# A one-core adaLN block: doubled weights loaded in 21 pieces, wider accumulations, and a new step table

## The chip, the core and the metric

The kernel runs on one core of a Trainium2 chip. The core has a matrix engine (PE, with its weight loads shown apart as PEld), a vector engine (DVE), a scalar engine (ACT), a general engine (POOL) and a sync engine (SP) that here only issues transfers; sixteen DMA engines move the data. SBUF and PSUM have 128 partitions. The metric is the device time of one execution, in microseconds; a kernel's time is the median of its runs. A profile is one execution of its own with the profiler on. Its span runs from the first to the last instruction, and the execution's own time is a little longer.

## The reference

Sequence length S = 2048, width D = 448, 16 heads of 28, F/2 = 896, everything in bf16. Two mixers follow each other, each on a modulated layer norm, each added to x through a gate:

```python
sa, ca, ga, sb, cb, gb = split(silu(c) @ w_mod, 6)
h = layernorm(x) * (1 + ca) + sa
q, k, v = heads(h @ wqkv)
phi_q = concat(softmax(q @ w_phi), softmax(-(q @ w_phi)))    # phi_k alike
kv = einsum('bhsf,bhsd->bhfd', phi_k, v);  z = einsum('bhsf->bhf', phi_k)
o = (phi_q @ kv) / (phi_q @ z + 1e-06)
x = x + ga * (o @ wo)
h = layernorm(x) * (1 + cb) + sb
y = gelu(h @ w_in);  z1, z2 = y[:, :896], layernorm(y[:, 896:])
x = x + gb * ((z1 * (w_sp @ z2 + b_sp)) @ w_out)
```

w_sp is 2048 x 2048, w_in 448 x 1792, w_out 896 x 448.

## The kernel before

The 2048 rows are 16 tiles of 128, mostly handled as 8 pairs. D = 448 is 7 blocks of 64. A transposed pair (hT) holds, for each block, the first tile's 64 features in partitions 0 to 63 and the second tile's in 64 to 127. A matmul of a pair is therefore two matmuls of 64 rows, one in each half of PE's rows (HALF[0], HALF[1]), and the weights against which hT runs (k, q, v weights, wo, w_in) must lie in SBUF twice, once in each half of the partitions. For wv, wo and the two halves of w_in (y and z) `load_half` fetches the whole matrix into 64 partitions, and is called twice for each, so there are eight such transfers: wv0, wv1, wo0, wo1, wy0, wy1, wz0, wz1.

Nothing schedules the kernel but a table, the string ORDER: some 860 words, each a step with its arguments, engine (/Y is SP, /S ACT, /V DVE, /G POOL) and PSUM slot (@). `fast_path` runs through it and issues the steps' instructions. Each engine runs its instructions in that order, and where one waits, everything behind it on that engine waits too. Loads are words as well (ld:x1/Y). SP issues almost all transfers, so its share of ORDER is the order of the loads, of the DMA transposes (T1 for the first norm's output, T2 for the attention's output, T3 for the second norm's, W for w_sp) and of the output.

The stages that matter here, in their order:

- cf computes modulation columns with matmuls of one column (L776), ec copies them from PSUM; FT, ET, PF, EP fold w_phi into the q and k weights.
- l1s to l1a norm x; X and XE (first two pairs) or T1 and md transpose and modulate it into hT.
- The k loop, for pairs 0 to 7: kM multiplies by the k weights, kE takes both exponentials (ACT, L878), kS sums them (DVE), kR takes reciprocals, kP scales (DVE or POOL, L895), vM multiplies by wv, vC copies the result, kA adds phi_k^T v into one PSUM accumulator over all pairs (L905). kA runs the two 64-row halves as separate matmuls into two banks; kb (ACT, L910) copies the second bank to SBUF and kc (DVE, L913) adds the first, adds the small constant, and km writes the block-diagonal KVbd. qM and qE do the queries, in between.
- gr and ge make the gates ga and gb as rows; wos and wts multiply wo and w_out by them (`gate`, L947), some blocks at a time, on DVE or POOL.
- For each tile nM (PE, L960), nX, nC, nS, nV, nT (DVE, L980, into f_t, which has two buffers) divide by the normalizer; nA (POOL or DVE, L986) adds the two parts into f_oo; T2 transposes it; wX and wM (PE, L997, L1005) multiply by wo and add x; wR, wQ, lA, lD, l2r, l2a norm again; T3 transposes.
- zM (L1056) and yM (L1073) multiply by w_in, pM and its helpers do the spatial product with w_sp, oM and oE the output.
- du, dh and dk are matmuls of zeros that keep PE busy while it has nothing to do.

```python
    def load_half(eng, dst, src, h):
        eng.dma_start(out=dst[HALF[h]], in_=src.rearrange("(k p) n -> p k n", p=HB))
```

Of the kernel before, what the change touches and what calls it, by code (L numbers as in the profile page):

```python
# [9 lines left out]
ALU = mybir.AluOpType  # L10
# [5 lines left out]
P = 128  # L16
# [467 lines left out]
ld:wq/Y ld:c/S du:6@1 ld:phi/Y ld:wk/S ld:x1/Y tbl ld:x2/Y du:6@1 ld:wsa/Y ld:x0/Y ld:x3/Y du:2@1 ld:wca/Y FTq:0@0 bd:0/V ld:x4/Y m5 ct@1 bd:1/V FTq:1@2  # L484
ce:1 ETq:0/S ETq:1/V FTk:1@3 FTk:0@4 ce:2 l1s:1 ETk:1/S PFq:4@C ce:3 l1s:2 ETk:0/S l1e:1,2/G PFq:6@A1 du:2@0 l1r:1,2 ce:4 EPq:5/S l1s:3 PFk:0@A2 EPq:6/S m4
PFk:4@A0 l1s:0 l1a:1/G EPq:4/S cf:0@2 EPk:4/S l1e:2,4/V l1e:0,1/V PFq:2@C ld:wsb/Y EPk:0/S l1r:0,1 l1s:4 PFk:6@A0 du:2@3 ld:x5/Y l1a:0/G EPk:6/S l1s:5
PFk:2@A2 ld:wv1/Y EPq:3/S l1r:2,4 cf:1@3 ld:wv0/Y l1s:7 EPk:2/S l1a:3/G X:0@0 ec:0 ec:1 EPq:2/S l1s:6 PFq:0@A2 l1a:2/G ld:wcb/Y XE:0,2,4/S du:1@2 XE:0,4,6/V
scb X:1@1 XE:0,6,7/S XE:0,0,2/V l1e:4,8/G XE:1,0,2/S cf:2@2 XE:1,6,7/V l1r:4,8 l1s:8 XE:1,4,6/S kM:0@C ec:2 l1s:9 EPq:0/S l1a:5/G XE:1,2,4/S l1s:13 l1a:7/G
kE:0,1 kM:1@A1 l1a:4/G l1s:10 EPq:1/S l1a:6/G T1:2,3 l1s:11 kE:0,0 qM:0@A0 m7 l1s:12 m3 kE:1,1 T1:3,4 l1e:8,12/G kS:0,0,2 kE:1,0 qM:1@A2 l1r:8,12 ld:wmgb/Y
qE:0,0 ld:wmga/Y l1a:8/G vM:0@C kS:1,0,2 qE:0,1 l1a:10/G l1a:11/G vM:1@A1 vC:0/S l1a:9/G T1:5,6 l1s:15 qE:1,1 md:0,2,4,6,7/G cf:3@0 kR:0,0,2 md:0,2,4,1,2/G  # L490
T1:4,5 md:0,2,4,4,5/V md:0,2,4,2,3/S md:0,2,4,0,1/G md:0,2,4,3,4/V gr:1@1 md:0,2,4,5,6/S kP:0,0/G l1s:14 vC:1/S ld:wout/Y gr:0@6 W:0,0 l1e:12,16/V qE:1,0
kR:1,0,2 kM:2@A1 kP:0,1/V l1r:12,16 ge:0 kP:1,1/V kP:1,0/V md:0,4,6,6,7/G qM:2@A2 kE:2,0 l1a:15/V m6 kE:2,1 ec:3 md:0,4,6,3,4/V l1a:13/G l1a:12/V kM:3@C
ge:1 l1a:14/G kS:2,0,2 md:0,4,6,1,2/S T1:6,7 qE:2,1 vM:2@A1 md:0,4,6,5,6/G md:0,4,6,0,1/G T1:7,8 kE:3,1 md:0,4,6,2,3/G vM:3@A0 md:0,4,6,4,5/V wts:4,6/G
kR:2,0,2 kE:3,0 ld:wo0/Y vC:2/S W:0,5 kS:3,0,2 kM:4@C qE:2,0 md:0,6,8,1,2/G ld:wz0/Y qM:4@A1 md:0,6,8,0,1/G kE:4,1 md:0,6,8,3,4/G wts:2,4/V kE:4,0 ld:wo1/Y
kA:0@A2 kR:3,0,2 md:0,6,8,5,6/S kA:1@A2 md:0,6,8,6,7/V kP:2,1/G kS:4,0,2 vC:3/S kM:5@C qE:4,0 ld:wz1/Y vM:4@A0 md:0,6,8,2,3/G qE:4,1 kP:2,0/V md:0,6,8,4,5/G
# [39 lines left out]
def fast_path(tc, A_x, A_wqkv, A_w_phi, A_wo, B_w_in, B_w_sp, B_b_sp, B_w_out, c, w_mod, out, flag):  # L535
# [119 lines left out]
    def load_half(eng, dst, src, h):  # L655
        eng.dma_start(out=dst[HALF[h]], in_=src.rearrange("(k p) n -> p k n", p=HB))
# [252 lines left out]
    def kb():  # L909
        nc.scalar.copy(out=kvb, in_=ps["kv"][:, 1, 0:464])  # L910
# [394 lines left out]
```

## Time and profile before

| | us |
|---|---|
| median of 2 runs (267.71 to 267.81) | 267.76 |
| the profiled execution | 265.91 |
| its span | 264.1 |
| PE busy in the span | 238.7 |
| DVE busy | 185.0 |
| POOL busy | 127.3 |
| ACT busy | 113.7 |
| share of the span that SP's DMA queue fills on 16 engines | 51.9% |
| first kE (ACT, L878) | 23.8 |
| kb (ACT, L910) | 66.4 |
| first nA (POOL, L986) | 73.4 |
| first wM (PE, L1005) | 78.4 |
| first zM (PE, L1056) | 99.6 |

In the lines of the profile L12 is line 12 of the kernel. A group's line names line, engine, operation, the tile written and the tiles read, the count, the busy time and the mean. A line of waits names the waiting engine and line, what released it, the total, the number of times and the longest. "issue" means that the engine waited for nothing that the profile shows. A line of windows gives the stretch, the busy time of PE, PEld, DVE, ACT and POOL with instruction counts, the granted PE clock (1 is full), the busy share of the DMA engines and the GB/s they moved.

### The profile page before, as it was taken

How to read it: one execution, taken by the hardware profiler on the slowest of the kernel's cores; microseconds unless marked ns; L12 is line 12 of the kernel's file. 1: busy time of each engine (PE TensorE's matmuls, PEld its weight loads, DVE VectorE, ACT ScalarE, POOL GpSimd, SP SyncE). 2: the span in 40 equal slices, each digit the busy share in tenths (PEclk: the TensorE clock that was granted, in tenths of full speed). 3: DMA queues.
4: the chain of work that ended last, by engine and by line, in shares of the span. 5: the costliest groups of instructions: out<-in, count | busy, mean ns of one | idle time of the engine just before them, and what ended most of it. 6: DMA issues, size and time to landing. Idle time of an engine off the chain costs nothing.

```text
span 264.1 us, 6349 instructions
## 1 busy us (share of the span) xinstructions
PE 238.7 (90%) x2631; PEld 135.5 (51%) x2640; DVE 185.0 (70%) x354; ACT 113.7 (43%) x209; POOL 127.3 (48%) x147
## 2 busy tenths in 40 slices
PE   8887999993888878999799999999999999999990
PEld 6664756573864543544356544444444444544550
DVE  1955989892799977688446997449758968156650
ACT  3945899971827656799597730000001000000000
POOL 1677696970075876538447708705305281222000
PEclk9965999997959997999999999999999999999997
DMA  7998969999014795679940100009993000100032
GB/s 203 314 240 142 224 130 159 200 193 167 2 37 72 112 155 105 108 133 179 181 90 0 35 7 0 0 1 171 171 193 63 20 17 17 55 0 2 0 116 69
DMA packets 67782, 26.97 MB, mean 102 GB/s; under 512 B 55585, under 2 KB 67618, under 8 KB 67746
## 3 DMA queue, kind: packets, MB, share of 16 engines
q1 hardware_dynamic: 66992, 25.98, 51.9%
q10 hardware_dynamic: 754, 0.52, 0.7%
q8 instruction: 22, 0.36, 0.6%
q14 instruction: 14, 0.11, 0.1%
HBM read 11.22 MB, written 1.84 MB: 49 GB/s over the span
## 4 chain that ended last, share of the span: by engine, by line
PE 63%; DVE 8%; DMA 6%; POOL 6%; issue 6%; SPq 5%; ACT 4%; DVEq 0%; ACTq 0%; POOLq 0%
PE f_psum L1153 27%; PE f_psum L1103 8%; PE f_psum L1090 5%; DMA f_hx<-f_hx 5%; PE f_psum L1073 5%; PE f_psum L1056 4%; SPq L1082 3%; PE f_psum L871 3%; PE f_psum L929 3%; POOL f_hx L794 2%; PE f_psum L1005 2%; DMA f_phi<-in_A_w_phi_dram 2%; DVE f_t L980 2%; POOL f_hx L847 1%; DVE f_ksum L888 1%
## 5 line engine op out<-in xcount | busy, mean ns | idle before, releaser
L1205 POOL TENSOR_TENSOR f_z1T<-f_win,f_z1T 128x512 bf16<-128x512 f32 x10 | 13.7, 1377 | 34.2 <-DVE f_win L1180 34.2
L1153 PEld LDWEIGHTS <-f_z2n 128*128 128x128 bf16 x192 | 18.7, 98 | 22.0
L1056 PE MATMUL f_psum<-f_win,f_hx 64*128 64x448 bf16 x224 | 24.6, 368 | 3.8 <-DVE f_hx L794 1.4
L1153 PE MATMUL f_psum<-f_wsp,f_z2n 128*128 128x512 bf16 x116 | 27.3, 379 | 0.2
L1173 ACT ACTIVATE f_Eq<-f_psum 128x512 f32<-128x512 f32 x4 | 2.4, 597 | 47.8 <-PE f_psum L1153 47.8
L986 POOL TENSOR_TENSOR f_oo<-f_t 128x448 bf16<-128x448 bf16 x12 | 12.3, 1033 | 21.1 <-DVE f_t L980 21.1
L1153 PE MATMUL f_psum<-f_hx,f_Eq 128*128 128x512 bf16 x93 | 21.7, 379 | 0.2
L1073 PE MATMUL f_psum<-f_hx,f_win 64*128 64x512 bf16 x196 | 21.8, 376 | 0.0
L1103 PE MATMUL f_psum<-f_wout,f_z1T 128*128 128x448 bf16 x105 | 21.3, 352 | 0.0
L1180 DVE SCALAR_TENSOR_TENSOR f_win<-f_psum,f_win 128x512 f32<-128x512 f32 x22 | 14.7, 685 | 9.3 <-PE f_psum L1153 9.2
L1056 PEld LDWEIGHTS <-f_hx 64*128 64x128 bf16 x224 | 11.7, 98 | 15.9 <-issue 3.0
L935 ACT ACTIVATE f_Eq<-f_psum 128x1024 bf16<-128x1024 f32 x16 | 16.1, 1034 | 7.2 <-PE f_psum L929 7.2
L888 DVE TENSOR_REDUCE f_ksum<-f_E 128x64 f32<-128x1792 bf16 x8 | 15.9, 2004 | 4.4 <-ACT f_E L878 4.4
L929 PE MATMUL f_psum<-f_hx,f_Wq 64*128 64x256 bf16 x224 | 14.3, 276 | 4.3 <-issue 4.3
L871 PEld LDWEIGHTS <-f_hx 64*128 64x128 bf16 x224 | 11.6, 99 | 12.7 <-issue 4.2
L980 DVE TENSOR_TENSOR f_t<-f_psum,f_w 128x896 bf16<-128x896 f32 x16 | 16.7, 1086 | 0.4
L1073 PEld LDWEIGHTS <-f_win 64*128 64x128 bf16 x196 | 12.0, 94 | 9.1
L794 POOL TENSOR_SCALAR f_hx<-f_hx,f_mod 128x256 bf16<-128x256 bf16 x19 | 13.1, 701 | 7.0 <-DMA f_hx<-f_hx 7.0
L871 PE MATMUL f_psum<-f_Wk,f_hx 64*128 64x448 bf16 x112 | 14.4, 398 | 1.8 <-DVE f_st L835 1.6
L1176 POOL TENSOR_TENSOR f_win<-f_Eq,f_bsp 128x512 f32<-128x512 f32 x4 | 7.0, 1759 | 18.5 <-ACT f_Eq L1173 18.5
L1061 ACT ACTIVATE f_z2n<-f_psum 128x896 bf16<-128x896 f32 x16 | 14.4, 908 | 3.2 <-PE f_psum L1056 3.2
L878 ACT ACTIVATE f_E<-f_psum 128x896 bf16<-128x896 f32 x16 | 14.0, 924 | 3.6 <-PE f_psum L871 3.5
(175 smaller groups left out, 511.0 us busy)
## 6 DMA issues: line engine op xcount, KB each, us to landing
f_win<-in_B_w_in_dram SPq DMA_DIRECT2D x4, 784.0 KB, 12.7
out_dram<-f_hx SPq DMA_DIRECT2D x15, 112.0 KB, 1.8
f_wm<-in_w_mod_dram SPq DMA_DIRECT2D x4, 392.0 KB, 6.2
f_x<-in_A_x_dram SPq DMA_DIRECT2D x3, 448.0 KB, 7.3
f_wv<-in_A_wqkv_dram SPq DMA_DIRECT2D x2, 392.0 KB, 9.1
f_ka<-in_w_mod_dram SPq DMA_DIRECT2D x2, 392.0 KB, 4.8
f_wout<-in_B_w_out_dram SPq DMA_DIRECT2D x1, 784.0 KB, 5.5
f_win<-in_A_wo_dram SPq DMA_DIRECT2D x2, 392.0 KB, 7.7
```

Source lines behind the costliest of these rows:

```text
L794: eng.tensor_scalar(out=out_, in0=in_, scalar1=sc, scalar2=sh, op0=ALU.mult, op1=ALU.add)
L871: nc.tensor.matmul(t[:, h, 0:n], lhsT=hT[HALF[h], p, j, :], rhs=w[HALF[h], j, 0:n], start=(j == 0), stop=(j == NB - 1))
L888: nc.vector.tensor_reduce(out=ksum[:, 2 * p + t0:2 * p + t1], in_=Er[:, p % NR, t0:t1].rearrange("p t a s (f h) -> p (t a s) h f", h=2), a ...
L929: nc.tensor.matmul(t[:, h, u * 256:(u + 1) * 256], lhsT=Wq[HALF[h], j, 2 * c2 + u].rearrange("p h e -> p (h e)"), rhs=hT[HALF[h], 2 * st:2 ...
L935: nc.scalar.activation(out=Eq[st // 2][:, 2 * c2:2 * c2 + 2, s, o:o + 512].rearrange("p u (h q) -> p h u q", h=2), in_=ps["q" + str(n)].re ...
L980: nc.vector.tensor_tensor(out=tr[i % 2].rearrange("p s (k h d) -> p k s h d", k=2, h=8), in0=numv(i)[:, :, :, :, 0:DH], in1=wr[i // 2 % 2] ...
L1056: nc.tensor.matmul(ps["z" + str(2 * p + h)][:, hf, 0:D], lhsT=hT[HALF[h], p, j, :], rhs=win[1][HALF[h], j, hf * D:(hf + 1) * D], start=(j ...
L1061: nc.scalar.activation(out=g, in_=ps["z" + str(i)][:, :, 0:D], func=ACT.Gelu_apprx_tanh, accum_out=zs1[:, i:i + 1])
L1073: nc.tensor.matmul(t[:, h, :], lhsT=win[0][HALF[h], j, fc * P:(fc + 1) * P], rhs=hT[HALF[h], 4 * g:4 * g + 4, j, :], start=(j == 0), stop= ...
L1103: nc.tensor.matmul(ps["o" + str(t)][:, 0, 0:D], lhsT=later["z1T"][:, fc, t * P:(t + 1) * P], rhs=wout_s[:, fc, :], start=(fc == 0), stop=( ...
L1153: nc.tensor.matmul(t[:, 0, :], lhsT=b[:, j, f * P:(f + 1) * P], rhs=a[:, j, :], start=(PSTART[k] and j == 0), stop=(j == NH - 1), skip_gro ...
L1180: nc.vector.scalar_tensor_tensor(out=out_, in0=bank_, scalar=ZR, in1=other, op0=ALU.mult, op1=ALU.add)
```

## The change

It has these parts.

- Loads. `load_half` is replaced by `load_twice`: one transfer for each 64-row block of a weight, written to all 128 partitions, its source read twice through a leading dimension of 2 with step zero. wv and wo are 7 pieces each (v0 to v6, o0 to o6, 448 columns), w_in 7 pieces over y and z at once (u0 to u6, 1,792 columns): 21 transfers for 8. f_win is laid out anew for it: wo first, then y and z side by side for each block.
- kA runs one matmul of 128 rows for two of 64, in one bank: 128 matmuls for 256. kb and kc's sum are gone; kc adds the constant in PSUM, km reads PSUM.
- cf takes windows of two blocks where it can: 32 matmuls for 56, four times; ec copies two halves, 8 operations for 4.
- The zero tile is 512 wide for 256 and du's matmuls are 512 columns wide; there are 9 for 19. dk has 99 matmuls for 183. dh's 8 are gone.
- ORDER is another table. Some steps change engines (one of kP from POOL to DVE, two zQ from DVE to ACT, two cX to POOL, and the like); loads, W transposes and slots stand elsewhere.
- Four new helpers (X2, XF, X3, XO) are defined and not used by the table.

```diff
-    def load_half(eng, dst, src, h):
-        eng.dma_start(out=dst[HALF[h]], in_=src.rearrange("(k p) n -> p k n", p=HB))
+    def load_twice(eng, dst, src, k):
+        v = src[k * HB:(k + 1) * HB]
+        eng.dma_start(out=dst[:, k, :], in_=v.unsqueeze(0).to_broadcast([2, HB, v.shape[1]]))
...
+    for k in range(NB):
+        LOADS["v%d" % k] = lambda q, k=k: load_twice(q, wv, A_wqkv[:, 2 * D:3 * D], k)
+        LOADS["o%d" % k] = lambda q, k=k: load_twice(q, wo_s, A_wo, k)
+        LOADS["u%d" % k] = lambda q, k=k: load_twice(q, wyz, B_w_in, k)
...
-            nc.tensor.matmul(wps[:, 0, 0:256], lhsT=zero[:, 0:P], rhs=zero[:, 0:256], start=True, stop=True)
+            nc.tensor.matmul(wps[:, 0, :], lhsT=zero[:, 0:P], rhs=zero[:], start=True, stop=True)
...
-        for j in range(NB):
+        for w in range(NB + 1):
+            rows = HALF[1] if w == 0 else HALF[0] if w == NB else slice(0, P)
+            a, b = max(0, w - 1), min(NB, w + 1)
             for kk in range(KC):
-                for h in range(2):
-                    nc.tensor.matmul(t[HALF[h], 0, j:j + 1], lhsT=wm1[:, kk, o + j * HB:o + (j + 1) * HB], rhs=scol[:, kk:kk + 1],
-                                     start=(kk == 0), stop=(kk == KC - 1))
+                nc.tensor.matmul(t[rows, 0, w:w + 1], lhsT=wm1[:, kk, o + a * HB:o + b * HB], rhs=scol[:, kk:kk + 1], start=(kk == 0), stop=(kk == KC - 1))
...
-                for h in range(2):
-                    nc.tensor.matmul(ps["kv"][:, h, a * 58:(a + 1) * 58], lhsT=PRT[HALF[h], p % NF, t, 2 * a:2 * a + 2, :].rearrange("p a e -> p (a e)"),
-                                     rhs=VRT[HALF[h], p % NR, t, 2 * a:2 * a + 2, :].rearrange("p h f -> p (h f)"),
-                                     start=(p == 0 and t == 0 and a == 0), stop=(p == NPR - 1 and t == 1 and a == 7), skip_group_check=True)
-
-    def kb():
-        nc.scalar.copy(out=kvb, in_=ps["kv"][:, 1, 0:464])
+                nc.tensor.matmul(ps["kv"][:, 0, a * 58:(a + 1) * 58], lhsT=PRT[:, p % NF, t, 2 * a:2 * a + 2, :].rearrange("p a e -> p (a e)"),
+                                 rhs=VRT[:, p % NR, t, 2 * a:2 * a + 2, :].rearrange("p h f -> p (h f)"),
+                                 start=(p == 0 and t == 0 and a == 0), stop=(p == NPR - 1 and t == 1 and a == 7), skip_group_check=True)
 
     def kc():
-        nc.vector.tensor_tensor(out=kvb, in0=ps["kv"][:, 0, 0:464], in1=kvb, op=ALU.add)
-        z = kvb.rearrange("p (a f) -> p a f", f=29)[:, :, 28]
+        z = ps["kv"][:, 0, 0:464].rearrange("p (a f) -> p a f", f=29)[:, :, 28]
         nc.vector.tensor_scalar(out=z, in0=z, scalar1=0.5e-6, scalar2=None, op0=ALU.add)
```

Of the table, the loads of the middle of the k loop show how it reads (a row before and one now):

```diff
-kP:3,1/V kE:5,1 kA:2@A2 kM:6@A1 kR:4,0,2 kE:5,0 kP:3,0/V kP:4,1/G vC:4/S kS:5,0,2 vM:5@C kE:6,0 ld:wy1/Y kM:7@A0 kE:6,1 kP:4,0/G kR:5,0,2 vC:5/S kS:6,0,2
+kP:3,1/G ld:u0/Y kS:5,0,2 kM:6@C qE:4,1 W:0,5 wts:6,7/G kA:2@4 kE:6,1 kR:4,0,2 kA:3@4 kP:4,1/V ld:u6/Y vC:5/S kM:7@A0 kP:4,0/V kE:6,0 kR:5,0,2 ld:o0/Y
```

What SP issues before, from w_out to the first transposes of f_oo (T2); f_wsp receives blocks of w_sp, f_hx is transposed by T1, f_win holds wo and w_in:

```order
L685 DMA f_wout<-in_B_w_out_dram 128x7x448
L1082 DMA_TRANSPOSE f_wsp_84<-in_B_w_sp_dram 128x8x128
L854 DMA_TRANSPOSE f_hx<-f_hx 128x7x128 x2
L656 DMA f_win<-in_A_wo_dram 64x7x448
L1082 DMA_TRANSPOSE f_wsp_84<-in_B_w_sp_dram 128x8x128
L656 DMA f_win<-in_B_w_in_dram 64x7x896
L656 DMA f_win<-in_A_wo_dram 64x7x448
L656 DMA f_win<-in_B_w_in_dram 64x7x896 x2
L1082 DMA_TRANSPOSE f_wsp_84<-in_B_w_sp_dram 128x8x128
L656 DMA f_win<-in_B_w_in_dram 64x7x896
L854 DMA_TRANSPOSE f_oo<-f_oo 128x7x128 x4
```

And now, from the last four T1 to the same place:

```order
L856 DMA_TRANSPOSE f_hx<-f_hx 128x7x128 x4
L687 DMA f_wout<-in_B_w_out_dram 128x7x448
L658 DMA f_win<-in_B_w_in_dram 128x1x1792 x3
L688 DMA f_bsp<-in_B_b_sp_dram 128x2048
L1096 DMA_TRANSPOSE f_wsp_84<-in_B_w_sp_dram 128x8x128
L658 DMA f_win<-in_B_w_in_dram 128x1x1792 x2
L658 DMA f_win<-in_A_wo_dram 128x1x448
L658 DMA f_win<-in_B_w_in_dram 128x1x1792
L1096 DMA_TRANSPOSE f_wsp_84<-in_B_w_sp_dram 128x8x128
L658 DMA f_win<-in_B_w_in_dram 128x1x1792
L658 DMA f_win<-in_A_wo_dram 128x1x448
L856 DMA_TRANSPOSE f_oo<-f_oo 128x7x128 x2
```

All of wv and five pieces of wo stand ahead of these rows; the last piece of wo, o0, is the last load ahead of the transposes of the attention's output, and the load of f_bsp has moved here from the second half.

What POOL does before between the k loop (f_qa is kP's output) and the sums of nA (f_oo):

```order
L895 TENSOR_TENSOR f_qa<-f_E,f_kr_121 128x16x56 x2
L947 TENSOR_TENSOR f_win<-f_win,f_g_rep 128x896
L895 TENSOR_TENSOR f_qa<-f_E,f_kr_122 128x16x56
L947 TENSOR_TENSOR f_win<-f_win,f_g_rep 128x448
L986 TENSOR_TENSOR f_oo<-f_t 128x7x64 x2
```

And now, with kP at L914, the gate at L961 and nA at L1000:

```order
L914 TENSOR_TENSOR f_qa<-f_E,f_kr_122 128x16x56
L961 TENSOR_TENSOR f_win<-f_win,f_g_rep 128x896
L914 TENSOR_TENSOR f_qa<-f_E,f_kr_121 128x16x56
L961 TENSOR_TENSOR f_win<-f_win,f_g_rep 128x896
L961 TENSOR_TENSOR f_wout<-f_wout,f_g_rep 128x896
L961 TENSOR_TENSOR f_win<-f_win,f_g_rep 128x896
L1000 TENSOR_TENSOR f_oo<-f_t 128x7x64 x5
```

The second row of f_win (wos:0,2) needs the pieces o0 and o1 of wo, and POOL reaches the first nA only behind it and two further scalings.

More of the change, by code (lines that the diff above doesn't have):

```diff
@@ L528 @@
[L528 to L531 removed]
+ld:x2/Y ld:c/S m5 m4 du:4@1 ld:phi/Y ld:wk/S ld:wq/Y tbl ld:x1/Y ld:x0/Y du:2@1 ld:x3/Y ld:wca/Y l1s:3 ct@0 du:2@2 ld:wsa/Y ce:1 l1s:2 FTk:1@1 ce:2
@@ new lines @@
+kP:0,0/V qE:2,0 T1:7,8 kP:0,1/V kM:3@A0 kP:1,1/V kE:2,0 kP:1,0/V T1:6,7 qE:2,1 kA:0@4 kS:2,0,2 cf:3@5 md:0,4,6,2,3/G md:0,4,6,0,1/S ld:wout/Y md:0,4,6,3,4/G
+kE:3,0 ld:u4/Y gr:0@6 md:0,4,6,4,5/G ld:u3/Y md:0,4,6,1,2/V kE:3,1 md:0,4,6,6,7/V cf:2@7 ld:u2/Y kR:2,0,2 md:0,6,8,6,7/G vC:3/S md:0,4,6,5,6/V kA:1@4
+md:0,6,8,2,3/G kS:3,0,2 ld:bsp/Y kM:4@A0 md:0,6,8,0,1/G md:0,6,8,4,5/S md:0,6,8,3,4/G ge:0 md:0,6,8,1,2/G kM:5@A1 kP:2,1/V kE:4,0 W:0,4 ec:2 kP:2,0/V kE:4,1
+wos:6,7/V vM:4@C ld:u1/Y wts:4,6/V kE:5,0 kR:3,0,2 ec:3 qM:4@A0 kE:5,1 wts:0,2/V kP:3,0/G ld:u5/Y kS:4,0,2 md:0,6,8,5,6/S vC:4/S vM:5@A1 ld:o1/Y qE:4,0
@@ L532 @@
+cX:1,2,21/G pM:1,2,3@4 cA:1,0,12 cA:1,0,21 cX:1,0,21/G pM:1,1,3@6 cA:1,2,12 cX:1,2,12/G gM:2,6@0 cA:1,1,12 cX:1,0,12/V cX:1,0,22/V gM:3,6@1 gG:2,6
+cX:1,1,12/V oM:9,0,7@6 oM:10,0,7@0 oE:9 gG:3,6 oM:8,0,7@6 read gG:4,6 oH:15,1@1 oE:8 oM:13,0,7@3 oE:10 oD:8/Y oD:9/Y oD:6/Y oD:10/Y oM:14,0,7@2 oM:12,0,7@0
+oE:14 oE:13 oH:15,0@5 oD:13/Y oE:12 oD:14/Y oM:11,0,7@4 oD:12/Y oG:15,0 oG:15,1 oF:15,0/S oF:15,1/S oE:11 oD:11/Y hint
 """
@@ L560, in fast_path @@
     ident = persist.tile([P, P], BF, name="f_ident")
-    zero = persist.tile([P, 256], BF, name="f_zero")
+    zero = persist.tile([P, 512], BF, name="f_zero")
     x_sb = persist.tile([P, NT, D], BF, name="f_x")
@@ L566, in fast_path @@
     W1 = NB * FH
-    wbig = persist.tile([P, 2 * W1 + NB * D], BF, name="f_win")
-    win = [wbig[:, u * W1:(u + 1) * W1].rearrange("p (k n) -> p k n", k=NB) for u in range(2)]
-    wo_s = wbig[:, 2 * W1:].rearrange("p (k n) -> p k n", k=NB)
+    W0 = NB * D
+    wbig = persist.tile([P, W0 + 2 * W1], BF, name="f_win")
+    wo_s = wbig[:, 0:W0].rearrange("p (k n) -> p k n", k=NB)
+    wyz = wbig[:, W0:].rearrange("p (k n) -> p k n", k=NB)
+    win = [wyz[:, :, u * FH:(u + 1) * FH] for u in range(2)]
     wout_s = persist.tile([P, FC, D], BF, name="f_wout")
@@ L733, in dh @@
         for _ in range(n):
-            nc.tensor.matmul(wps[:, 0, 0:256], lhsT=zero[:, 0:P], rhs=zero[:, 0:256], start=True, stop=True)
+            nc.tensor.matmul(wps[:, 0, :], lhsT=zero[:, 0:P], rhs=zero[:], start=True, stop=True)
     def dk(n, c0, slot):
@@ L782, in ec @@
     def ec(u):
-        dst, src = mods[u // 2][:, u % 2, :], ps["cf%d" % u][:, 0, 0:NB]
-        if u % 2:
-            nc.vector.tensor_scalar(out=dst, in0=src, scalar1=1.0, scalar2=ROOT[u // 2], op0=ALU.add, op1=ALU.mult)
-        else:
-            nc.vector.tensor_copy(out=dst, in_=src)
+        for h in range(2):
+            dst, src = mods[u // 2][HALF[h], u % 2, :], ps["cf%d" % u][HALF[h], 0, 1 - h:NB + 1 - h]
+            if u % 2:
+                nc.vector.tensor_scalar(out=dst, in0=src, scalar1=1.0, scalar2=ROOT[u // 2], op0=ALU.add, op1=ALU.mult)
+            else:
+                nc.vector.tensor_copy(out=dst, in_=src)
     def modulate(eng, out_, in_, u, j):
@@ L862, in X, with X2, XF, X3 @@
             nc.tensor.transpose(t[:, j * P:(j + 1) * P], xpad[:, p % NX, j, :], ident[:])
+    def X2(p, slot):
+        t = ps["X2_" + str(p)] = bank_bf(slot, "xt_ps")
+        for j in range(NB):
+            nc.tensor.transpose(t[:, j * P:(j + 1) * P], xpad[:, (NPR + p) % NX, j, :], ident[:])
+    def XF(p, j0, j1, eng):
+        for j in range(j0, j1):
+            modulate(eng, hT[:, p, j, :], ps["X2_" + str(p)][:, j * P:(j + 1) * P], 1, j)
+    def X3(p, slot):
+        t = ps["X3_" + str(p)] = bank_bf(slot, "xt_ps")
+        for j in range(NB):
+            nc.tensor.transpose(t[:, j * P:(j + 1) * P], opad[:, p % NO, j, :], ident[:])
+    def XO(p, eng):
+        copy_on(eng, oT[:, p % NO], ps["X3_" + str(p)][:, 0:NB * P].rearrange("p (k e) -> p k e", k=NB))
     def XE(p, j0, j1, eng):
```

106 lines of the change are left out of this document (46 added, 60 removed).

## The prediction

> **What bounds the kernel now.** I read the page's slices first, because a mean over stages hides which engine sets which stage, then the waits of PE, then the loads and the stages in which they run.
>
> ```profile
> span 264.1 us, 6349 instructions
> PE 238.7 (90%) x2631; PEld 135.5 (51%) x2640; DVE 185.0 (70%) x354; ACT 113.7 (43%) x209; POOL 127.3 (48%) x147
> PE   8887999993888878999799999999999999999990
> PEclk9965999997959997999999999999999999999997
> DMA  7998969999014795679940100009993000100032
> ...
> PE f_psum L929 <- issue: 4.3, 1, 4.3
> PE f_psum L776 <- issue: 2.2, 1, 2.2
> PE f_psum L871 <- DVE f_st L835: 1.6, 1, 1.6
> PE f_psum L1056 <- DVE f_hx L794: 1.4, 1, 1.4
> ```
>
> A slice is 6.6 us. PE is at 9 from the seventeenth slice on: the second half is matmul work, and the change leaves those matmuls alone. What can be won or lost lies in the first 110 us. There DMA is at 7 to 9 for ten slices, and the two largest waits of PE are put down to "issue": PE waits for nothing that the profile shows, while DMA is full. Now the loads (KB of one, median us to landing), and the stages in which they run (busy us of each engine, granted clock, DMA share, GB/s).
>
> ```profile
> f_win<-in_B_w_in_dram SPq DMA_DIRECT2D x4, 784.0 KB, 12.7
> f_wm<-in_w_mod_dram SPq DMA_DIRECT2D x4, 392.0 KB, 6.2
> f_x<-in_A_x_dram SPq DMA_DIRECT2D x3, 448.0 KB, 7.3
> f_wv<-in_A_wqkv_dram SPq DMA_DIRECT2D x2, 392.0 KB, 9.1
> f_ka<-in_w_mod_dram SPq DMA_DIRECT2D x2, 392.0 KB, 4.8
> f_wout<-in_B_w_out_dram SPq DMA_DIRECT2D x1, 784.0 KB, 5.5
> f_win<-in_A_wo_dram SPq DMA_DIRECT2D x2, 392.0 KB, 7.7
> f_bsp<-in_B_b_sp_dram SPq DMA_DIRECT2D x1, 512.0 KB, 5.3
> ...
> 0.00:6.60 6.60, 5.38 (x46) 4.04 (x47) 1.11 (x7) 2.43 (x4) 0.74 (x7) 1.00 0.78 203
> 6.60:13.20 6.60, 5.30 (x181) 4.41 (x180) 6.33 (x25) 6.60 (x12) 4.33 (x10) 1.00 1.09 313
> 26.40:40.00 13.60, 13.60 (x215) 9.18 (x212) 12.26 (x21) 12.37 (x17) 11.16 (x16) 1.00 0.97 175
> 52.00:60.00 8.00, 7.38 (x179) 5.30 (x176) 7.79 (x10) 5.71 (x7) 5.28 (x4) 1.00 1.17 192
> ...
> 11.00:14.00 3.00, 1.14 (x36) 0.88 (x36) 2.11 (x7) 2.40 (x5) 2.79 (x5) 1.00 1.07 326
> ```
>
> Rows into all partitions reach 326 GB/s over sixteen engines, 20.4 for each; in 52 to 60 us, when the half-partition loads of w_in run, 192 or 12.0 for each. Loading over all partitions, as the change does, is right on that point.
>
> **The loads in pieces.** The eight half-partition loads become 21. Each of the 14 pieces of wv and wo moves 64 rows of 896 bytes twice, each of the 7 of w_in 64 rows of 3,584 bytes twice: the same bytes in all. But the source of a piece begins with a dimension of two copies with step zero, and its rows come second. How a transfer is dealt out to the DMA engines decides the price. Three rows bear on that.
>
> ```profile
> q10 hardware_dynamic: 754, 0.52, 0.7%
> f_ka<-in_A_wqkv_dram ACTq DMA_DIRECT2D x1, 392.0 KB, 4.4
> out_dram<-f_hx ACTq DMA_DIRECT2D x2, 56.0 KB, 2.4
> f_c_row<-in_c_dram ACTq DMA_DIRECT2D x1, 0.9 KB
> ```
>
> ACT's queue q10 carries only these four transfers: 448 rows of 896 bytes for f_ka, two times 128 rows of 448 bytes, one row for c, together 705 packets. The 49 left over are 3 times 16 and 1, as if each engine that took part closed its share with one packet: sixteen for each transfer whose leading dimension is 112 or 128, one for the one whose leading dimension is 1. So the leading count seems to set the number of engines. The broadcast itself is not the trouble: f_bsp is a zero-step source too, with 128 copies in front, and its 512 KB land in 5.3 us, 99 GB/s, more than four engines at 20.4 give. With two copies in front, only two engines would share a piece, and that is my likeliest case. The Trainium skill, page "DMA: Bandwidth & Descriptors", section "Why a DMA increments its semaphore by 16 and not by 1", says that the number of engines is the largest up to 16 that divides the slowest dimension of both sides, and its "Rules for kernel authors" name a leading zero-stride broadcast of c copies as confined to c engines; the count of 49 agrees, while no load here has a leading 2.
>
> Price. Each of the two engines moves 14 x 64 x 896 + 7 x 64 x 3,584 = 2,408,448 bytes. The ends for one engine are 12.0 GB/s (201 us) and 20.4 (118 us) by the rows; nothing excludes more, since those rows are of sixteen engines that press the same memory, and the whole rows go better than the halves. I take the fast end and a tenth more, 22.4 GB/s, for fourteen idle neighbours: 107.5 us. The Trainium skill, same page, section "Specifications", gives about 27 GiB/s for an engine; by that figure the pieces would take an estimated 83 us; no row here shows an engine that fast.
>
> Where the queue stands. Before the first piece SP and ACT load 3,328 KB (x but for its last 448 KB, phi, q and k weights, three of the six 392 KB blocks of w_mod), 3.41 MB; the first two stages moved 203 x 6.6 + 313 x 6.6 = 3.41 MB, so the pieces start at 13.2 us. Whatever else SP issues between the first piece and the last, o0, has a sixteenth of itself on each of the two engines: the last of x, three w_mod blocks, wout and bsp, 2,920 KB at 326 GB/s, 9.2 us; six transposes of f_hx at 229 KB and two of w_sp at 262 KB, 1.9 MB at the 175 of the stage with such work, 10.9 us. So o0 lands at 13.2 + 107.5 + 9.2 + 10.9 = 140.8 us.
>
> Who waits for it. POOL scales wo's last rows and two more pieces by the gate, then adds the two halves of each head group (L986 before), whose sums go through T2 to the matmuls with wo.
>
> ```profile
> L947 POOL TENSOR_TENSOR f_wout<-f_wout,f_g_rep x2: 1034/1458/1881, 38.8 to 75.4; 128x896 bf16<-128x896 bf16 x1, 128x448 bf16<-128x448 bf16 x1
> L986 POOL TENSOR_TENSOR f_oo<-f_t x12: 1028/1032/1040, 73.4 to 102.7; 128x448 bf16<-128x448 bf16 x12
> L1005 PE MATMUL f_psum<-f_win,f_oo x112: 349/349/577, 78.4 to 109.7; 64*128 64x448 bf16 x112
> L980 DVE TENSOR_TENSOR f_t<-f_psum,f_w x16: 1080/1082/1093, 72.2 to 102.5; 128x896 bf16<-128x896 f32 x16
> ```
>
> POOL works in its order, so those three scalings of 128x896 at 1.88 us come after o0, and the first sum starts at 140.8 + 5.6 = 146.4 us; before it started at 73.4. From there the old kernel needed 264.1 - 73.4 = 190.7 us. f_t has two buffers, so only two of L980's products can run ahead, 2 x 1.08, say 2 us. The span is 146.4 + 190.7 - 2 = 335.1 us.
>
> **What lies under that wait.** vM waits for all seven pieces of wv, to about 33 us (13.2, 17.9 for 401,408 bytes each, 1.4 for x), with vM:1, qM:1 and kM:2 behind it on PE. The last transposes of f_hx stand behind seven wv and five wo pieces, so at 13.2 + 30.7 + 5.1 + 7.9 = 57 us; four tile pairs of the k loop follow, half of the loop that ran from its first exponential at 23.83 to kb at 66.4, 43 us, so to about 79 us. That is 67 us ahead of the first sum, so these costs, the steps handed from POOL to DVE and the other loads' order add nothing. Under the same cover, and worth nothing while it lasts, are the gains:
>
> ```profile
> 23.83 0.03 ACT f_E L878
> ...
> L739 PEld LDWEIGHTS <-f_zero x183: 92/95/128, 70.3 to 95.0; 64*128 64x128 bf16 x183
> L910 ACT COPY f_t<-f_psum x1: 546/546/546, 66.4 to 66.4; 128x464 f32<-128x464 f32 x1
> L913 DVE TENSOR_TENSOR f_t<-f_psum,f_t x1: 642/642/642, 67.0 to 67.0; 128x464 f32<-128x464 f32 x1
> 14.35 0.77 PE f_psum L776 x39
> 64.67 1.54 PE f_psum L905 x60
> ```
>
> Without the cover, kb and kc's sum are 0.55 + 0.64 = 1.2 us on the path, since km can only follow them. cf loses 96 matmuls at 0.77/39 = 20 ns, 1.9 us, off the path unless the columns are late; ec's four extra halves give back 0.6 at most. kA has 128 matmuls for 256: at 1.54/60 = 26 ns the gain would be 3.3 us, but pairs of 64 rows may run side by side, which makes it nothing; I take nothing. The fillers (dk 183 to 99, fewer but wider du, no dh) stand where PE waits for others; their end is the clock, 0.5 to 0.6 in some slices already, and they cost or bring under 2 us.
>
> **The second half** keeps its matmuls. wM:5 now stands behind zM:0 and twelve W transposes behind the last T2 instead of eleven; no wait of PE there is longer than the 1.4 us of L1056. I take zero, and 2 us either way.
>
> **The sum against the clock.** The profiled execution took 265.91 us, 1.8 more than its span, and the median of the runs, 267.76, is 1.85 above that: 3.7 to add to the span. 335.1 + 3.7 = 339 us.
>
> **Rivals.** First, the pieces are dealt to all sixteen engines, by their destination's 128 partitions. Then no load is late, half-partition rates are gone, and the three PE waits of 4.3, 2.2 and 1.6 us, which fall in slices with DMA at 8 or 9, go with kb and kc's sum: 9.3 us, 267.8 - 9.3 = 258 us, faster by 3.5%. For it speaks that the destination is full; against it the count of 49 packets. It decides at once: with eight engines the pieces would cost 27 us and be hidden by the loop.
>
> Second, all engines are used but the issue waits stay, because the same bytes fill the same 60 us: only the 1.2 us come, 266 to 267 us, the same.
>
> Third, two engines, and each no faster than in the half-partition loads: 12.0 GB/s, 201 us of pieces, 93 more, 432 us. Against it: the halves were slow with all sixteen engines writing to 64 partitions, where a pair has more room.
>
> **How the numbers follow.** Two engines at between 16 and 28.8 GB/s (as far above 20.4 as 12.0 is below it) has 0.79, the third rival 0.06, the first 0.11, the second 0.04. At 16 GB/s the pieces take 151 us, 43 more, 382; at 28.8 they take 84, 24 less, 315. The time given is the likeliest's, 339; 310 to 385 holds about eight in ten with nothing of the other sign. Faster by over 2%, about what a measurement of this kernel can tell from no change, 0.11; within 2% 0.04; slower 0.85.
>
> **What would show it.** Pieces of w_in that take 10 us each to land, one after another, with a DMA share near 2/16 from 60 to 140 us, and POOL and PE idle there; T2 at about 147 us; from then on the old second half. If instead the DMA rows show 300 GB/s for the pieces and zM starts before 95 us, the first rival is right. If the wait ends long before 140 us, the rate of one engine is what I had wrong.

## The result, and the profile after

| | before | after |
|---|---|---|
| median, us | 267.76 | 330.75 (329.0 to 332.49, 2 runs) |
| ratio to before, 95% interval | | 1.235 [1.207, 1.263] |
| span of the profiled execution | 264.1 | 330.6 |
| PE busy in it | 238.7 | 238.7 |
| first nA (POOL) | 73.4 | 140.8 |
| first wM (PE) | 78.4 | 145.8 |
| first zM (PE) | 99.6 | 166.7 |

Some executions of a kernel run in a slower state, at a lower granted clock; ratios here and below compare the others alone, medians are of all executions, and the profiles of e6 and e8 are of slower ones.

The changed kernel is slower by 63 us: 339 was predicted, within 310 to 385. PE does as much as before; it stands still in between. The page of the changed kernel, its slices now 8.3 us long:

```profile
span 330.6 us, 5700 instructions
PE   8961695799510000058689999999999989999992
PEclk9996597699855555559979999999999999999997
DMA  8836369519121911043788778081036800100012
GB/s 217 201 93 62 82 162 106 157 51 118 51 64 51 64 63 51 13 85 60 113 107 167 122 135 113 2 160 30 2 67 112 142 0 0 56 16 28 2 58 78
```

Before, no slice of PE between the tenth and the last fell below 7 (the row stands in the prediction). Now the thirteenth to seventeenth slice hold nothing, with the clock down to 0.5. In the eleventh to sixteenth DMA moves 51 to 64 GB/s; before, with loads of any kind, it moved 130 and more in each of the first ten slices:

```profile
GB/s 203 314 240 142 224 130 159 200 193 167 2 37 72 112 155 105 108 133 179 181 90 0 35 7 0 0 1 171 171 193 63 20 17 17 55 0 2 0 116 69
```

The waits of all engines name what is late, and the chain of waits shows how it ends (start, us, what):

```profile
ACT f_Sx L978 <- PE f_psum L974: 60.2, 6, 55.2
POOL f_win L961 <- DMA f_win<-in_A_wo_dram: 56.1, 1, 56.1
DVE f_t L994 <- POOL f_oo L1000: 53.0, 1, 53.0
...
119.38 0.53 SPq L658
119.91 0.04 issue
119.95 15.23 DMA f_win<-in_A_wo_dram
135.19 0.02 issue
135.23 0.09 issue
135.32 1.87 POOL f_win L961
137.19 1.83 POOL f_wout L961
139.02 1.83 POOL f_win L961
140.85 1.00 POOL f_oo L1000
```

POOL waits 56.1 us for one load, the last piece of wo; DVE waits for POOL, since f_t has two buffers, PE waits for DVE, and ACT for PE. o0 lands at 135.2, POOL scales three pieces, and nA begins. What SP issued, from the first piece to the first transposes of f_oo:

```profile
13.02 3.65 SPq L658 DMA_DIRECT2D f_wv<-in_A_wqkv_dram  x3
...
46.64 10.91 SPq L856 DMA_TRANSPOSE f_hx<-f_hx  x4
57.60 0.58 SPq L687 DMA_DIRECT2D f_wout<-in_B_w_out_dram  x1
58.23 10.32 SPq L658 DMA_DIRECT2D f_win<-in_B_w_in_dram  x3
68.59 9.34 SPq L688 DMA_DIRECT2D f_bsp<-in_B_b_sp_dram  x1
77.98 10.76 SPq L1096 DMA_TRANSPOSE f_wsp<-in_B_w_sp_dram  x1
88.78 3.51 SPq L658 DMA_DIRECT2D f_win<-in_B_w_in_dram  x2
92.34 5.86 SPq L658 DMA_DIRECT2D f_win<-in_A_wo_dram  x1
98.25 4.08 SPq L658 DMA_DIRECT2D f_win<-in_B_w_in_dram  x1
102.37 16.96 SPq L1096 DMA_TRANSPOSE f_wsp<-in_B_w_sp_dram  x1
119.38 0.53 SPq L658 DMA_DIRECT2D f_win<-in_B_w_in_dram  x1
119.95 2.66 SPq L658 DMA_DIRECT2D f_win<-in_A_wo_dram  x1
142.85 3.15 SPq L856 DMA_TRANSPOSE f_oo<-f_oo  x2
```

The second column is the time that the issue took. The issue of a piece takes 0.53 us at 119.38 and that of a W transpose 1.30 at 146.06; before that, the longest of a piece takes 9.16 us and that of a W transpose 16.96. SP seems to stand before a queue that takes no more; no row names what holds it. So POOL's wait, from 79.2 to 135.3 us, has two parts: until 119.95 SP has not issued o0, and the 15.23 us after that are its landing. Last, windows of the changed kernel, the first and third with the pieces alone, the second with a W transpose among them (DMA share and GB/s are the last two columns):

```profile
69.00:78.00 9.00, 9.00 (x150) 5.81 (x146) 8.76 (x10) 6.87 (x9) 5.32 (x4) 1.00 0.14 51
105.00:117.00 12.00, 0.00 (x0) 0.00 (x0) 0.00 (x0) 0.00 (x0) 0.00 (x0) 0.50 1.11 61
119.00:136.00 17.00, 0.00 (x0) 0.00 (x0) 0.00 (x0) 0.00 (x0) 0.68 (x1) 0.50 0.15 51
```

A share of 0.14 to 0.15 of sixteen engines is 2.2 to 2.4 of them, and 51 GB/s over two engines is 25.5 for each.

There is a second, exact sign in the count of packets of SP's queue, before and now:

```profile
q1 hardware_dynamic: 66992, 25.98, 51.9%
```

```profile
q1 hardware_dynamic: 66010, 25.98, 46.2%
```

The data rows of the changed loads fall from 8 x 448 = 3,584 to 21 x 128 = 2,688, by 896. If every transfer ends with one packet for each engine that took part, as the prediction read from ACT's queue, the eight old loads closed with 8 x 16 = 128 and the pieces with 21 x 2 = 42, by 86 fewer: 982 in all, and 66,992 - 982 is 66,010. With sixteen engines for each piece it would be 66,304.

### The profile page after: what moved, and what is told of

The parts are those of the page before. It is cut to its first block, busy times and chain, and to the rows that moved or that the text cites. A ratio compares the mean times of both kernels' runs of the same rounds, so it can differ in the third digit from the quotient of the medians.

```text
span 330.6 us, 5700 instructions
## 1 busy us (share of the span) xinstructions
PE 238.7 (72%) x2305; PEld 128.3 (39%) x2314; DVE 187.2 (57%) x352; ACT 112.1 (34%) x205; POOL 132.2 (40%) x155
## 3 DMA queue, kind: packets, MB, share of 16 engines
q1 hardware_dynamic: 66010, 25.98, 46.2%
## 4 chain that ended last, share of the span: by engine, by line
PE 46%; SPq 29%; DMA 14%; POOL 4%; DVE 3%; issue 2%; ACT 0%; ACTq 0%; DVEq 0%; POOLq 0%
PE f_psum L1167 18%; SPq L658 11%; SPq L1096 10%; PE f_psum L1087 6%; PE f_psum L1070 6%; PE f_psum L1117 6%; DMA f_win<-in_A_wo_dram 5%; PE f_psum L1104 4%; SPq L856 3%; DMA f_wv<-in_A_wqkv_dram 3%; SPq L688 3%; DMA f_oo<-f_oo 2%; PE f_psum L1019 2%; DMA f_Eq<-in_B_w_sp_dram 2%; SPq L668 1%
## 5 line engine op out<-in xcount | busy, mean ns | idle before, releaser
L974 PE MATMUL f_psum<-f_KVbd,f_Eq 56*128 56x60 bf16 x256 | 6.7, 193 | 49.6 <-DVE f_t L994 48.9
L961 POOL TENSOR_TENSOR f_win<-f_win,f_g_rep 128x896 bf16<-128x896 bf16 x3 | 5.6, 1875 | 56.1 <-DMA f_win<-in_A_wo_dram 56.1
L974 PEld LDWEIGHTS <-f_Eq 56*128 56x128 bf16 x256 | 5.7, 98 | 52.1 <-issue 51.3
L1070 PE MATMUL f_psum<-f_win,f_hx 64*128 64x448 bf16 x224 | 23.7, 368 | 2.8 <-POOL f_hx L796 2.8
L1219 POOL TENSOR_TENSOR f_z1T<-f_win,f_z1T 128x512 bf16<-128x512 f32 x9 | 12.2, 1367 | 30.1 <-DVE f_win L1194 30.1
L890 PEld LDWEIGHTS <-f_hx 64*128 64x128 bf16 x224 | 12.9, 105 | 29.0 <-issue 19.0
L890 PE MATMUL f_psum<-f_wv,f_hx 64*128 64x448 bf16 x112 | 14.4, 404 | 12.4 <-DMA f_wv<-in_A_wqkv_dram 12.4
L978 ACT COPY f_Sx<-f_psum 128x32 f32<-128x32 f32 x16 | 2.7, 184 | 60.3 <-PE f_psum L974 60.2
L1187 ACT ACTIVATE f_win<-f_psum 128x512 f32<-128x512 f32 x2 | 1.2, 597 | 48.6 <-DVE f_z1T L1219 44.7
L1070 PEld LDWEIGHTS <-f_hx 64*128 64x128 bf16 x224 | 11.2, 98 | 14.5 <-POOL f_hx L796 2.9
```

What stands on the lines that cost most here:

```text
L890: nc.tensor.matmul(t[:, h, 0:n], lhsT=hT[HALF[h], p, j, :], rhs=w[HALF[h], j, 0:n], start=(j == 0), stop=(j == NB - 1))
L1070: nc.tensor.matmul(ps["z" + str(2 * p + h)][:, hf, 0:D], lhsT=hT[HALF[h], p, j, :], rhs=win[1][HALF[h], j, hf * D:(hf + 1) * D], start=(j ...
```

## The experiments

Times are medians of two or more runs; a kernel is compared with runs of the kernel before on its own chip, which gave medians of 267.25, 266.34 and 268.65 us in the three groups (e1 to e4, e5 to e7, e8 and e9).

| run | what | us | ratio, 95% interval |
|---|---|---|---|
| e1 | after, 4 copies in front | 287.28 | 1.075 [1.064, 1.086] |
| e2 | after, 16 copies in front | 259.24 | 0.971 [0.962, 0.979] |
| e3 | after, 42 transfers without broadcast | 266.89 | 0.998 [0.994, 1.002] |
| e4 | after, wo's pieces first | 321.6 | 1.204 [1.190, 1.217] |
| e5 | before, with the pieces alone | 319.68 | 1.199 [1.186, 1.212] |
| e6 | after, old half loads on two queues | 263.28 | 0.987 [0.980, 0.994] |
| e7 | before, with kA's matmuls alone | 264.11 | 0.991 [0.987, 0.995] |
| e8 | after, old half loads on SP | 262.3 | 0.988 [0.977, 0.998] |
| e9 | after, 42 transfers on two queues | 275.06 | 1.037 [1.023, 1.051] |

### Is the leading count the number of engines? e1 and e2

The transfers keep their number, order, bytes and length of rows; only the source's first dimension changes, from 2 x 64 rows to 4 x 32 and 16 x 8. With 4 copies half of the rows of the weights are left out, with 16 seven eighths.

```diff
-        v = src[k * HB:(k + 1) * HB]
-        eng.dma_start(out=dst[:, k, :], in_=v.unsqueeze(0).to_broadcast([2, HB, v.shape[1]]))
+        v = src[k * HB:k * HB + 32]
+        eng.dma_start(out=dst[:, k, :], in_=v.unsqueeze(0).to_broadcast([4, 32, v.shape[1]]))
```

> The kernel after, but each of the 21 pieces loads the first 32 of its 64 rows four times, so its source has 4 copies in front instead of 2; the same number of transfers, rows of the same length, the same bytes, the same order. Half of the rows of wv, wo and w_in are thereby left out of the computation. Theory (the leading count is the number of DMA engines): the two engines moved 51 GB/s between 119 and 136 us, so four move twice that and the pieces' 94 us become 47; o0 lands near 88 us instead of 135, and 330.8 becomes 284 us (278 to 292). Rival 1 (what costs is 21 transfers on SP, not the engines): 328 to 333. Rival 2 (a zero step that reads the same rows again is slow in itself): not faster than 328.

> As the last, with 8 rows of each piece loaded sixteen times: 16 copies in front, the same transfers and bytes. Seven eighths of the rows of wv, wo and w_in are left out of the computation. Theory: sixteen engines share each piece, nothing waits for the pieces, and the time is that of the rest of the change, 258 us (253 to 264), faster than before. Rivals 1 and 2: 328 or more. It also shows what the first rival of the prediction would have given, and whether PE's waits put down to issue are gone (theory of the prediction) or stay (266 to 267).

With 4 copies the time is 287.3 us, with 16 it is 259.2. The theory said 284 and 258; both rivals said 328 or more. The packets follow it to the last one. SP's queue in e1, then in e2:

```profile
q1 hardware_dynamic: 66052, 25.98, 51.0%
```

```profile
q1 hardware_dynamic: 66304, 25.98, 50.7%
```

66,052 is 66,010 - 42 + 21 x 4, and 66,304 is 66,010 - 42 + 21 x 16. The landing of o0 moves as it should too. The chain of e1:

```profile
78.31 11.08 DMA f_win<-in_A_wo_dram
...
89.53 1.87 POOL f_win L961
```

o0 has landed at 89.4 instead of 135.2, 45.8 us earlier, where halving 94.4 us of pieces gives 47. So the number of copies in front sets the number of engines, and neither the number of transfers nor the repeated reading costs the 63 us.

e2 also shows what time the first rival of the prediction would have come to, 259 us for 258. Its waits of PE:

```profile
PE f_psum L974 <- DVE f_t L994: 4.4, 5, 2.2
PE f_psum L1070 <- POOL f_hx L796: 2.4, 1, 2.4
PE f_psum L923 <- POOL f_qa L914: 1.5, 2, 1.1
```

The waits of 4.3 and 2.2 us put down to issue don't appear, so the condition of the second rival, that they stay, does not hold here. But they are absent from e3, e6, e8 and e9 as well, which load half partitions with the table after. So loads over all partitions are not needed for that.

### What waits behind the pieces? e4

```diff
-ld:u4/Y
+ld:o1/Y ld:o0/Y ld:u4/Y
```

The two words go away at their old places.

> The kernel after, with the last two pieces of wo (o1, o0) ahead of the pieces of w_in. What holds the sums of nA, POOL's scaling of wo, then has its data by 60 us. Theory A (every transfer on SP has its share on the two engines, behind what was issued before): T2 of the first pair still lands only behind all of w_in, near 136 us, the first matmul with wo starts near 137 instead of 145.8, and the time is 320 to 325 us. Theory B (only POOL's wait on o0 counts): the attention output is ready from about 95 us on, the next to wait is the first zM on w_in at 135 instead of 166.7, and the time is 295 to 303 us.

It took 321.6 us, 9 less than the changed kernel, in the range of theory A. POOL no longer waits for wo, the first nA starts at 90.1, and then:

```profile
PE f_psum L1019 <- DMA f_oo<-f_oo: 33.0, 2, 32.7
```

PE, at wM, waits for the transpose of f_oo. SP's rows show where that transfer was:

```profile
102.37 17.80 SPq L1096 DMA_TRANSPOSE f_wsp<-in_B_w_sp_dram  x1
120.22 0.53 SPq L658 DMA_DIRECT2D f_win<-in_B_w_in_dram  x1
120.85 11.00 SPq L856 DMA_TRANSPOSE f_oo<-f_oo  x2
```

The first two sums of f_oo were done at 92.1, but SP came to their transpose only at 120.8. The chain then gives it 13.5 us to land, where the changed kernel, with no piece ahead of it, shows 2.9. So some two thirds of the wait lie before the issue, with SP held at the loads and W transposes ahead, and one third behind it. Theory A had only the second part, the transfer's share on the two engines that still have pieces; that this is what the 13.5 us are fits, but the trace does not tell the engines apart. Moving the loads that are waited for to the front therefore brings little: here a transfer on few engines delays every later one of its queue.

### Do the pieces alone do it? e5

The table of before, with v0 to v6 at the places of wv0 and wv1, and so on, and f_win laid out as after.

> The kernel before with the loads alone changed: the 21 pieces with two copies in front, and the layout of f_win that they need, at the places of the eight half-partition loads; everything else as before. Theory (two engines, 25.5 GB/s each): 94 us of pieces from 11.3 us on and some 26 us of other transfers' shares between them put the last piece of w_in, and T2 behind it, near 132 us; the first matmul with wo starts near 135 instead of 78.4, and the time is 318 to 330 us. Rival (the slowdown needs the new table, which puts wo's last piece behind w_in): under 300 us.

319.68 us, as the theory had it. Its longest wait of PE:

```profile
PE f_psum L1007 <- DMA f_oo<-f_oo: 41.2, 2, 40.8
```

The new table is not needed for the slowdown; here too it ends in T2's wait, and here too SP issues T2 late, at 118.9 us. The changed kernel takes another 11 us. There o0 stands last and POOL's three scalings, 5.5 us, come behind it; the rest of the 11 is not split further.

### What is the rest of the change worth? e3, e6, e8, e9

All four have the whole computation and the table after. e3 replaces each piece by two transfers of 64 rows:

```diff
-        eng.dma_start(out=dst[:, k, :], in_=v.unsqueeze(0).to_broadcast([2, HB, v.shape[1]]))
+        for h in range(2):
+            eng.dma_start(out=dst[HALF[h], k, :], in_=v)
```

> The kernel after, with each piece as two transfers of 64 rows to 64 partitions each, without the broadcast: 42 transfers, the whole computation. Theory: each transfer has 64 in front on both sides and goes to all engines, so the pieces hide again: 256 to 264 us. Rival 1 (the number of transfers on SP costs): slower than 331, since the number doubles. Rival 2 (the zero step): also 256 to 264, so this run tells rival 1 alone apart.

266.89 us, above the range expected: the 63 us are gone, but so is the gain of e2. The packets are again those of 16 engines for 42 transfers (2,688 data rows and 672 closing packets where the pieces had 2,688 and 42):

```profile
q1 hardware_dynamic: 66640, 25.98, 51.3%
```

I took the loss for the half partitions, written one after the other, and tried the eight old loads with the upper halves on ACT's queue.

```diff
-ld:v1/Y ... ld:v2/Y ... ld:o5/Y ... ld:u4/Y ... ld:u1/Y
+ld:wv0/Y ld:wv1/S ... ld:wo0/Y ld:wo1/S ... ld:wy0/Y ld:wy1/S ... ld:wz0/Y ld:wz1/S
```

> The kernel after with the eight half-partition loads of before in place of the pieces, the lower halves issued by SP and the upper ones by ACT at the same places of the table (four issues for ACT), so that both halves of the partitions are written at the same time. Theory 1 (what keeps the two-halves kernel at 267 is that all engines write to 64 partitions at a time, about 200 GB/s): the loads run near 320 GB/s again and the time is that of the kernel with sixteen copies in front, 257 to 262 us. Theory 2 (it is the larger number of transfers on SP, or ACT's issues hold its own work up by as much): 264 to 270 us.

263.28 us, between the pieces in 42 transfers and the full loads, and in the gap between the ranges of the two theories. The control puts the four upper halves back on SP, and e9 gives ACT the upper halves of all 21 pieces.

> The two-queue kernel with its upper halves issued by SP again: the table after with the eight half-partition loads of before, all on SP. Theory 1 (writing both halves at the same time is what the second queue brings): 265 to 268 us, like the 42 transfers on SP. Theory 2 (fewer transfers on SP are what it brings): 261 to 264, like the two queues.

> The kernel after, each piece as two transfers of 64 rows, the lower half issued by SP and the upper by ACT right behind: 21 issues each, the whole computation. Theory 1 (both halves at once): the loads are as fast as with sixteen copies, but ACT's 21 issues of 0.55 us take 12 us of an engine that is at 9 tenths in the k loop; if they hide, 259 to 262 us, if they don't, 264 to 270. Theory 2 (the number of transfers): 266 or more.

e8 took 262.3 us: one queue is as good as two, as theory 2 had it, and theory 1's 265 is not reached, though e8's wide interval still touches it. The windows go the same way. In the stretch of the w_in loads, which also holds b_sp and two W transposes, e2 (full partitions), then e3, then e8:

```profile
35.00:57.00 22.00, 20.41 (x324) 13.50 (x324) 19.59 (x26) 16.08 (x22) 14.24 (x14) 1.00 1.08 210
```

```profile
42.00:64.00 22.00, 21.72 (x307) 13.65 (x304) 19.95 (x26) 17.75 (x23) 14.49 (x12) 0.88 1.08 223
```

```profile
37.00:60.00 23.00, 20.96 (x301) 13.09 (x301) 19.12 (x25) 15.89 (x21) 14.05 (x12) 0.93 1.09 199
```

All three move 199 to 223 GB/s, at a DMA share of 1.08 or 1.09. The full partitions bring no faster stream here, against what the prediction read from 326 and 192 GB/s. What differs between e8 and e3 is the number of transfers that SP issues, 8 and 42, and w_in's loads stand 5 us later in e3. That fewer issues are the cause fits, but only these two runs bear on it, and their intervals overlap. Nor does any run show whether e2's reading of eight rows sixteen times is itself worth something. e9 took 275.06 us, and its waits show a new one:

```profile
ACT f_E L898 <- DMA f_win<-in_B_w_in_dram: 9.5, 1, 9.5
```

ACT, which takes the exponentials of the k loop, stood 9.5 us, and its next rows are issues of w_in of its own. Theory 1's bad case came, and worse than its 270; theory 2's "266 or more" holds the time too, so this run does not decide between them.

e6 and e8 compute everything and are faster than the kernel before by 1.3 and 1.2%; e8's interval only just leaves out no change, and neither shows as much as 2% with certainty. So the rest of the change is worth some 3 us with the old loads. e7 gives kA's part of it; the new table, cf and the fillers were not taken apart.

### kA alone: e7

```diff
-                for h in range(2):
-                    nc.tensor.matmul(ps["kv"][:, h, a * 58:(a + 1) * 58], lhsT=PRT[HALF[h], ...
+                nc.tensor.matmul(ps["kv"][:, 0, a * 58:(a + 1) * 58], lhsT=PRT[:, ...
```

with kb and kc's sum gone, in the kernel before.

> The kernel before with kA's 128-row matmuls alone, kb and kc's sum gone, the table otherwise as before. By the prediction's terms: kb and the sum are 1.2 us on the path, the matmuls themselves nothing, so 266 us (265 to 267). Rival: the 128 matmuls saved are worth their 26 ns each, 3.3 us more, 262 to 263. Rival: with 256 PE instructions fewer ahead of it, the 4.3 us wait at L929 moves or goes, 262 or less.

264.11 us, 0.9% less [0.5, 1.3], 2.2 us for the 1.2 expected, and by its median short of both rivals. The interval, 1.4 to 3.4 us, excludes the 1.2 only just. The waits of PE name what may be the rest:

```profile
PE f_psum L955 <- issue: 2.4, 1, 2.4
PE f_psum L776 <- issue: 2.3, 1, 2.3
```

The wait of 4.3 us at L929 is not there; one of 2.4 us put down to issue stands later, at nM (L955). With 128 matmuls and as many weight loads fewer ahead of it, it moved and was 1.9 us shorter. So this part of the change works. That the shorter wait is what it brings beyond the 1.2 us fits, but rests on one profile of each kernel, and what the wait is stays open.

## Why the prediction was right, point by point

**The mechanism**, that only two engines share a piece, is shown in three ways: the time and the landing of o0 follow the number of copies in front (e1, e2), the packets agree to the last one, and 51 GB/s move at a share of 0.14. The rule that the prediction named from the Trainium skill, page "DMA: Bandwidth & Descriptors", section "Why a DMA increments its semaphore by 16 and not by 1", that the slowest dimension of both sides sets the number of engines, agrees for 2, 4 and 16.

**Its terms.** The pieces were to start at 13.2 us; the first was issued at 13.0. wv was to be in by 33 us; the chain has PE start on it at 35.7. The last transposes of f_hx were to come at 57 us; SP left them at 57.55. The k loop was to end at about 79 us; its last kA ended at 81.5, so it did lie under the wait. o0 was to land at 140.8; it landed at 135.2, 5.6 us early, and that is nearly all that the sum was off before the second half. Two terms make it up, with opposite signs:

- The pieces. 22.4 GB/s for an engine was too low: at the 25.5 of the windows with the pieces alone, 2,408,448 bytes take an estimated 94.4 us instead of 107.5. One engine with idle neighbours moved a quarter more than its share of 326 GB/s. The direction of the step "a tenth more" was right, its size was not. The Trainium skill's figure of about 27 GiB/s, in the same page's section "Specifications", or 29.0 GB/s, is about as far above 25.5 as the 22.4 is below it.
- The rest of the queue. 135.2 - 13.0 - 94.4 leaves 27.8 us for what was put at 20.1. Which of it is the transposes' larger share and which is idle time of the two engines while SP stood before a W transpose stays open: the trace does not tell the engines apart.

That o0's landing was forecast so closely is partly luck: an error of 13.1 us and one of 7.7 cancel in part.

**From o0 on** the three scalings took 5.5 us (135.3 to 140.85), where 5.6 were predicted. From nA to the end it took 330.6 - 140.8 = 189.8 us; 190.7 less 2 for what could run ahead were predicted. From the first zM to the end it is 163.9 us, before 164.5: the second half is unchanged. The span came out 4.5 us below the 335.1 predicted. The other 3.6 us of the miss lie in what was added to the span: 3.7 us were added, and the median of two runs, one of them the profiled one at 332.49, stands only 0.15 above it.

**The share of DMA** near 2/16 was predicted for the whole stretch from 60 to 140 us. It holds where the pieces run alone; with transposes queued it was 0.74 over 78 to 103 us and 1.11 over 105 to 117, which is told below. POOL and PE were to be idle there: POOL was from 79 us on, PE, but for its matmuls of zeros, from 88 on.

**The rivals.** Sixteen engines gave 259.2 us (e2) for 258 predicted, but the agreement is luck, for its terms don't hold: the loads stay at about 210 GB/s where w_in comes, and the waits put down to issue are gone in e3 too, which yet took 266.9. The second rival's condition, that they stay, was false, though e3 has its time of 266 to 267. The third, 12.0 GB/s for an engine, fell at 25.5. The row of 192 GB/s from which it came, 52 to 60 us before, is not of half-partition loads alone:

```profile
46.08 8.54 SPq L1082 DMA_TRANSPOSE f_wsp<-in_B_w_sp_dram  x1
54.66 0.60 SPq L656 DMA_DIRECT2D f_win<-in_B_w_in_dram  x1
```

A W transpose was issued just ahead, and in e2, with full partitions, the stretch with two of them moved hardly more, 210 GB/s.

**kA.** Its 1.2 us were 2.2 in the kernel before; the likeliest term left out, not shown, is the wait put down to issue, which moved and shortened.

## What to carry to other kernels

Look at the first dimension on both sides of a transfer before its size: a broadcast whose copies stand in front was moved here by as many engines as there were copies, for 2, 4 and 16, and every later transfer of the queue was held up by it, however wide it was itself. Count the packets: data rows and one for each engine that took part, and the queue line of the profile shows how many engines a transfer had without a single duration. If a load must be doubled over the partitions, few large transfers, one for each half, do it: they took 262.3 us here, 42 small ones 266.9. Sixteen copies in front, which leave most rows out, took 259.2.

## What the runs showed of the hardware that was not expected

With a DMA transpose queued behind the pieces all engines looked busy while little moved. From 105 to 117 us, with a transpose of w_sp issued behind pieces that two engines were still working on, the share was 1.11 at 61 GB/s, against 0.14 at 51 from 69 to 78 us, and SP's issue of it took 16.96 us. A high share of DMA is therefore no sign of a full DMA; the GB/s beside it are needed.

Issuing can also hold up the engine that does it: on SP it delayed later loads and T2, which in e4 was issued 28.7 us after its sums were done, and on ACT in e9 it went with a stand of 9.5 us in the k loop.
